# Running sums of logs and angles: one fp32 product against products of ones with two 12-bit halves

## The chip, the cores and the metric

The kernel runs on one core of a Trainium2 chip. The metric is the time of one execution in device microseconds; three executions of the kernel before gave 684.42, 684.94 and 685.08 us, median 684.94. The profile shown is one further execution of 683.65 us, of which the profiler's span is 681.9 us. All times inside the kernel are microseconds from the start of that span.

## The reference

A gated linear attention with complex gates is followed by a layer of two matrix products around a gate h cos(h).

```python
# q, k, v, a_re, a_im: (4, 8, 768, 48) fp32; w_in: (384, 2048), w_out: (2048, 384)
mag = np.sqrt(a_re * a_re + a_im * a_im)
scale = np.minimum(mag, 0.999) / (mag + 1e-06)
a_re_n, a_im_n = (a_re * scale, a_im * scale)
for t in range(S):                       # S = 768 steps
    ar, ai = (a_re_n[:, :, t, :, None], a_im_n[:, :, t, :, None])
    new_re = ar * S_re - ai * S_im       # the state is turned and shrunk
    new_im = ar * S_im + ai * S_re
    kv = np.einsum('bhd,bhe->bhde', k[:, :, t], v[:, :, t])
    S_re, S_im = (new_re + kv, new_im)
    y[:, :, t] = np.einsum('bhd,bhde->bhe', q[:, :, t], S_re)
# (B,H,S,D) -> (B*S, H*D): x of 3072 x 384
h = x @ w_in
g = h * np.cos(h)
out = (g @ w_out).astype(np.float32)
```

## The kernel before

The 768 steps of a batch are cut into six chunks of C = 128 steps. Within a chunk the product of all gates up to a step is exp(running sum of log magnitudes), turned by the running sum of angles. Both running sums are matrix products with a triangle of ones, 128x128, against the chunk's 128x384 logs or angles. Two chunks make a group g; there are 24 chunks and 12 groups. Groups 0 and 1 (g < PEG) take one path, groups 2 to 11 the other, in which the rows of a chunk are stored turned by one step.

The names that the profile uses: `lg` are the logs, `tan` the angles, `lgs` and `phs` the running sums in PSUM, `P` (stored over `lg`) and `Q` their exponentials, `ks` and `qs` the rotated keys and queries, `sc` the scores, `sp` the new state, `yp` the attention output, `hp` the product with `w_in`, `op` and `sum` those with `w_out`.

```python
# the constants: a triangle of ones, and the same over pi, for each of the two paths
sums = [constant(sums_np[0], "sums")]
turns = [constant(sums_np[0] * np.float32(1.0 / math.pi), "turns")]
# ... (later, for g >= PEG)
sums.append(constant(sums_np[1], "sums_turned", nc.sync))
turns.append(constant(sums_np[1] * np.float32(1.0 / math.pi), "turns_turned", nc.sync))

# log_steps, its end: the last writes of the log and the angle, and a check of the sign of re
    special(out=rs, in_=rs, func=AF.Ln, scale=EPS, bias=one_b)
    special(out=sq, in_=mag, func=AF.Ln)
    special(out=sq, in_=sq, func=AF.Exp, scale=-1.0)
    vector.tensor_tensor(out=m2, in0=m2, in1=rs, op=ALU.subtract)        # m2 is lg
    vector.tensor_tensor(out=mag, in0=mag, in1=sq, op=ALU.mult)          # sq is tan
    vector.scalar_tensor_tensor(out=sq, in0=mag, scalar=2.0, in1=sq,
                                op0=ALU.subtract, op1=ALU.mult)
    vector.scalar_tensor_tensor(out=sq, in0=sq, scalar=-1.0, in1=im,
                                op0=ALU.mult, op1=ALU.mult)
    scalar.activation(out=junk, in_=re, func=AF.Relu, scale=-1.0, accum_out=...)

def p_powers(g, i):                       # one chunk of the logs
    ps = pa.tile([C, DM], F32, tag="a", name="lgs")
    matmul(ps, lhsT=sums[g >= PEG], rhs=cut(x["lg"], i, 1), start=True, stop=True)
    special(out=cut(x["P"], i, 1), in_=ps, func=AF.Exp)
    special(out=cut(x["Q"], i, 1), in_=ps, func=AF.Exp, scale=-1.0)

def p_even(g, i, n):                      # "mag<-Q,lg", "lg<-mag,lg", "Q<-mag,Q"
    vector.scalar_tensor_tensor(out=u, in0=Q, scalar=HUGE, in1=P, op0=ALU.min, op1=ALU.mult)
    for t in P, Q:
        vector.scalar_tensor_tensor(out=t, in0=u, scalar=3.0, in1=t,
                                    op0=ALU.subtract, op1=ALU.mult)
    # ... two DMAs

def p_apply(g, i, n):                     # "Q<-k,Q", "mag<-q,lg"
    vector.tensor_tensor(out=Q, in0=cut(x["k"], i, n), in1=Q, op=ALU.mult)
    vector.tensor_tensor(out=u, in0=cut(x["q"], i, n), in1=P, op=ALU.mult)

def g_carry(g, i):                        # the end of the chunk before, added to row 127
    n, some = g * G + i, ds(C - 32, 32)
    if g >= PEG and n % NCH:              # not where a batch begins
        head = cut(X[g]["tan"], i, 1)[some]
        vector.scalar_tensor_tensor(out=head, in0=before(n)[some], scalar=carry[some],
                                    in1=head, op0=ALU.mult, op1=ALU.add)

def g_phase(g, i):                        # one chunk of the angles
    ps = pa.tile([C, DM], F32, tag="a", name="phs")
    early = g < PEG and n % NCH
    if i:
        g_carry(g, i)
    matmul(ps, lhsT=turns[g >= PEG], rhs=cut(x["tan"], i, 1), start=True, stop=not early)
    if early:
        matmul(ps, lhsT=last, rhs=before(n), start=False, stop=True)
    ph = cut(x["tan"], i, 1)
    scalar.copy(out=ph.bitcast(I32), in_=ps)                             # whole turns
    vector.tensor_tensor(out=ph, in0=ps, in1=ph.bitcast(I32), op=ALU.subtract)
```

`prods` of a group runs p_powers for both chunks, the arctangent of the angles (g_angle), g_carry for the first chunk, then p_even and p_apply. `phases` runs g_phase for both chunks, `keys` the sines, the rotations and the transposes of keys and queries, which go through DMA to `kT` and `qT`. `weave` sets the program order: each part gives its pieces places between two fractions, and the pieces are sorted by them. Turn n of the main loop works on the chunks of group n, the products of groups n-1 and n, and prepares group n+1:

```python
for n in range(2, NG):
    weave((mixes(n - 1, 2, 4), 0.0, 0.12), (logs(n + 1), 0.0, 0.02), (chunks(n), 0.0, 0.36),
          (second(n - 1, 0), 0.0, 0.38), (products(n - 1, 0, 3), 0.0, 0.36),
          (prods(n + 1), 0.22, 0.24), (second(n - 1, 1), 0.4, 0.56),
          (products(n - 1, 3, 7), 0.4, 0.56), (phases(n + 1), 0.4, 0.56),
          (keys(n + 1), 0.53, 0.66), ..., (first(n), 0.56, 1.0), ...)
```

`first` is hp, `second` and `products` are op and sum, `chunks` holds sc, sp and yp. The scheduler keeps matmuls in the order of the program; on the other engines it decides.

Of the kernel before, what the change touches and what calls it, by code (L numbers as in the profile page):

```python
# [11 lines left out]
F32 = mybir.dt.float32  # L12
U8 = mybir.dt.uint8
U32 = mybir.dt.uint32
I32 = mybir.dt.int32
BF16 = mybir.dt.bfloat16
I64 = mybir.dt.int64
AF = mybir.ActivationFunctionType
ALU = mybir.AluOpType
# [467 lines left out]
def fast_path(ctx, tc, q, k, v, a_re, a_im, moe_w_in, moe_w_out, out, least, odd, wide):  # L487
# [41 lines left out]
    last_np[C - 1] = 1.0  # L529
    carry_np = np.where(step_np == C - 1, np.float32(math.pi), np.float32(0.0))[:, None]  # L530

    def constant(array, name, queue=nc.scalar):
        t = consts.tile(list(array.shape), F32, name=name)
        queue.dma_start(out=t, in_=nc.inline_tensor(array, name=name + "_const").ap())
        return t

# [31 lines left out]
    for names in ("re", "im"), ("k", "q"), "v":  # L568
        for i in range(G):
            load(0, names, i)  # L570
    ident = constant(np.eye(C, dtype=np.float32), "ident")
    sums = [constant(sums_np[0], "sums")]
    turns = [constant(sums_np[0] * np.float32(1.0 / math.pi), "turns")]
    last = constant(last_np, "last")
    carry = constant(carry_np, "carry")
    causal = constant(causal_np * np.float32(0.25), "causal")
    tiny_b = scalar_tile(TINY, "tiny_b")
# [70 lines left out]
    def chain(ins, engine="scalar"):  # L648

        if engine in tail:  # L650
            behind(ins, tail[engine])
        tail[engine] = ins
# [29 lines left out]
    def matmul(out, **kw):  # L682
        chain(nc.tensor.matmul(out, **kw), "tensor")  # L683
# [30 lines left out]
    def cut(t, i, n):  # L714
        return (flat(t) if len(t.shape) == 4 else t)[:, ds(i * DM, n * DM)]

    def log_steps(g, i, n):


        x = X[g]  # L720
        re, im = cut(x["re"], i, n), cut(x["im"], i, n)
        if i == 0:
            if g == 0:
                x["sin"] = temp("tan", 2)
            for name in "lg", "tan", "rs", "mag":
# [18 lines left out]
        yield  # L744
        vector.tensor_tensor(out=m2, in0=m2, in1=rs, op=ALU.subtract)
        yield
        vector.tensor_tensor(out=mag, in0=mag, in1=sq, op=ALU.mult)
        vector.scalar_tensor_tensor(out=sq, in0=mag, scalar=2.0, in1=sq,
                                    op0=ALU.subtract, op1=ALU.mult)
        vector.scalar_tensor_tensor(out=sq, in0=sq, scalar=-1.0, in1=im,  # L750
                                    op0=ALU.mult, op1=ALU.mult)
        yield
        junk = msb.tile([C, DM], BF16, tag="below", name="below", bufs=1) if n == 1 else rs
        scalar.activation(out=junk, in_=re, func=AF.Relu, scale=-1.0,
                          accum_out=odd[:, ds(next(odds), 1)])

    def g_log(g, i, n):
        for _ in log_steps(g, i, n):
            pass

    def p_powers(g, i):

        x = X[g]
        if i == 0:
            x["P"], x["Q"] = x["lg"], temp("Q")
            x["row"] = rows_d.tile([G * DM], F32, tag="row", name="row")
            x["end"] = ft.tile([D2, G * H], F32, tag="end", name="end")
        ps = pa.tile([C, DM], F32, tag="a", name="lgs")
        matmul(ps, lhsT=sums[g >= PEG], rhs=cut(x["lg"], i, 1), start=True, stop=True)
        special(out=cut(x["P"], i, 1), in_=ps, func=AF.Exp)  # L770
        special(out=cut(x["Q"], i, 1), in_=ps, func=AF.Exp, scale=-1.0)

# [34 lines left out]
    def before(n):  # L807
        return cut(X[(n - 1) // G]["tan"], (n - 1) % G, 1)

    def g_carry(g, i):  # L810

        n, some = g * G + i, ds(C - 32, 32)
        if g >= PEG and n % NCH:
            head = cut(X[g]["tan"], i, 1)[some]
            vector.scalar_tensor_tensor(out=head, in0=before(n)[some], scalar=carry[some],
                                        in1=head, op0=ALU.mult, op1=ALU.add)

    def g_phase(g, i):

        x, n = X[g], g * G + i  # L820
        ps = pa.tile([C, DM], F32, tag="a", name="phs")
        early = g < PEG and n % NCH
        if i:
            g_carry(g, i)
        matmul(ps, lhsT=turns[g >= PEG], rhs=cut(x["tan"], i, 1), start=True, stop=not early)
        if early:
            matmul(ps, lhsT=last, rhs=before(n), start=False, stop=True)
        ph = cut(x["tan"], i, 1)
        scalar.copy(out=ph.bitcast(I32), in_=ps)
        vector.tensor_tensor(out=ph, in0=ps, in1=ph.bitcast(I32), op=ALU.subtract)  # L830

# [298 lines left out]
    def prods(g):  # L1130
        if not 0 <= g < NG:
            return
        for i in range(G):
            yield lambda i=i: p_powers(g, i)
        yield lambda: g_angle(g, 0, G)
        yield lambda: g_carry(g, 0)
        yield lambda: (p_even(g, 0, G), p_apply(g, 0, G))

    def logs(g):
# [4 lines left out]
    def phases(g):  # L1144
        return [lambda i=i: g_phase(g, i) for i in range(G)] if 0 <= g < NG else []
# [15 lines left out]
    def second(g, i):  # L1161
        return [lambda j0=j0: mm2(g, i, j0, 4) for j0 in range(0, NJ, 4)] if g < PLAIN else []
# [19 lines left out]
    after = consts.tile([1, 1], F32, name="after")  # L1182
    wait_for(X[0]["im"][0:1, G - 1, 0, 0:1])
    load(1, ("re", "im", "k", "q"))
    sums.append(constant(sums_np[1], "sums_turned", nc.sync))
    turns.append(constant(sums_np[1] * np.float32(1.0 / math.pi), "turns_turned", nc.sync))
    early = [weight(dst, src) for dst, src in into[:RAW]]
    Ordered.by_hand = True
    preload("natural_log_exp_and_others")
    busy(12)  # L1190
# [20 lines left out]
    for t in (turned(0, 0, "kT") + turned(0, 0, "qT") + early[:1]  # L1211
# [13 lines left out]
          (logs(2), 0.3, 0.31), (chunks(1), 0.7, 1.0), (prods(2), 0.85, 0.87))  # L1225
    room.close()
    stage.update(pool=ctx.enter_context(tc.tile_pool(name="late", bufs=1)), bufs=1)
    weave((second(0, 1), 0.0, 0.35), (phases(2), 0.0, 0.1), (keys(2), 0.1, 0.4),
          (first(1), 0.4, 1.0))
    for n in range(2, NG):  # L1230
        weave((mixes(n - 1, 2, 4), 0.0, 0.12), (logs(n + 1), 0.0, 0.02), (chunks(n), 0.0, 0.36),
              (second(n - 1, 0), 0.0, 0.38), (products(n - 1, 0, 3), 0.0, 0.36),
              (prods(n + 1), 0.22, 0.24), (second(n - 1, 1), 0.4, 0.56),
              (products(n - 1, 3, 7), 0.4, 0.56), (phases(n + 1), 0.4, 0.56),
              (keys(n + 1), 0.53, 0.66), (quarters() if n == PLAIN else [], 0.4, 0.9),
              (last_quarter() if n == PLAIN else [], 0.9, 1.0), (first(n), 0.56, 1.0),
              (mixes(n, 0, 2), 0.9, 1.0), (guarded(n - 1, per) if n > 3 else [], 0.1, 0.9))
# [77 lines left out]
```

## Time and profile before

| what | value |
|---|---|
| median of three executions | 684.94 us |
| span of the profile | 681.9 us |
| mean granted TensorE clock | 0.987 |
| TensorE time of four lgs records (two products) in the chain | 1.29 us |
| ScalarE activation of 128x768, typical | 0.84 us |
| VectorE two-operand fp32 instruction of 128x768 | 0.95 us |
| VectorE carry, 32x384 | 0.618 us, 17 of them |
| hp of successive groups starts at (n=2 to 5) | 174.43, 225.55, 277.97, 328.77 us |

PE is TensorE's matmuls, PEld its weight loads, which overlap them; DVE is VectorE, ACT ScalarE, POOL GpSimd, SP the queue that issues most DMAs. A share of busy time is an average over the span. In lists of instructions a line gives the start, the duration, the engine, the operation with output and inputs, and in square brackets the time for which the engine stood idle before it and what it then waited for. The chain that ended last is followed back from the last instruction, at each step to what released it.

### The profile page before, as it was taken

The numbers are of one execution on the slowest core, as the hardware profiler recorded it, in microseconds if no ns is written. First come the engines' busy times: TensorE is split into PE (matmuls) and PEld (weight loads), VectorE is DVE, ScalarE is ACT, GpSimd is POOL, SyncE is SP. The second block draws the span as 40 slices with busy tenths as digits, with TensorE's granted clock in tenths as the row PEclk, the third lists the DMA queues.
The fourth block names the chain that finished last, engine by engine and source line by source line (L and its number), as shares of the span: only waits on it lengthen the run. The fifth ranks groups of instructions, "written<-read, shape, count | busy, mean of one in ns | idle before, by whom it ended". The sixth has DMA issues, their size and how long they took to land.

```text
span 681.9 us, 10685 instructions
## 1 busy us (share of the span) xinstructions
PE 653.7 (96%) x4060; PEld 577.7 (85%) x4060; DVE 480.3 (70%) x782; ACT 382.5 (56%) x710; POOL 27.3 (4%) x45
## 2 busy tenths in 40 slices
PE   5788999999999999999999999999999999999996
PEld 5686676886899889899899889999899889999895
DVE  4889988468867877777777777767777768762251
ACT  5769784473474475466476476366466467332330
POOL 2012000000000000000000000000000000000000
PEclk8979999999999999999999999999999999999998
DMA  9777717706537557656657657565766653264000
GB/s 245 177 232 230 187 59 159 201 1 143 160 70 140 153 126 164 170 131 154 184 127 158 180 128 161 158 145 122 205 139 130 196 128 83 104 141 127 24 6 24
DMA packets 232954, 94.97 MB, mean 139 GB/s; under 512 B 208814, under 2 KB 221361, under 8 KB 232892
## 3 DMA queue, kind: packets, MB, share of 16 engines
q1 hardware_dynamic: 226396, 68.68, 44.6%
q0 software_dynamic: 5632, 25.17, 11.0%
q8 instruction: 34, 0.56, 0.4%
q10 hardware_dynamic: 864, 0.33, 0.2%
q14 instruction: 28, 0.23, 0.1%
HBM read 69.35 MB, written 24.81 MB: 138 GB/s over the span
## 4 chain that ended last, share of the span: by engine, by line
PE 84%; DMA 5%; DVE 5%; ACT 4%; issue 1%; DVEq 0%; ACTq 0%
PE hp L683 31%; PE op L683 17%; PE sum L683 15%; PE sc L683 6%; PE yp L683 5%; PE sp L683 3%; PE lgs L683 2%; DMA raw<-in_moe_w_out_dram 2%; PE phs L683 2%; DMA qT<-moved 2%; DVE w_in L672 1%; ACT raw L672 1%; DVE w_out L672 1%; PE yr L683 1%; DMA im<-in_a_im_dram 1%
## 5 line engine op out<-in xcount | busy, mean ns | idle before, releaser
L683 PE MATMUL hp<-xT,w_in 128*128 128x256 f32 x1152 | 253.6, 382 | 0.6 <-ACT xT L672 0.6
L683 PEld LDWEIGHTS hp<-xT,w_in 128*128 128x128 f32 x1152 | 220.1, 191 | 32.2 <-ACT xT L672 1.0
L702 ACT ACTIVATE gate<-hp,half_pi_b 128x512 f32<-128x512 f32 x96 | 65.9, 687 | 126.6 <-PE hp L683 126.6
L672 DVE TENSOR_TENSOR gate<-hp,gate 128x512 f32<-128x512 f32 x96 | 65.6, 683 | 60.0 <-ACT junk L672 60.0
L683 PE MATMUL op<-w_out,gate 128*128 128x192 f32 (+1 forms) x448 | 101.6, 375 | 2.3 <-DVE w_out L672 2.3
L683 PEld LDWEIGHTS op<-w_out,gate 128*128 128x128 f32 x448 | 75.8, 190 | 22.5 <-DVE w_out L672 3.5
L672 ACT ACTIVATE junk<-hp 128x512 bf16<-128x512 f32 x96 | 56.6, 590 | 0.0
L683 PE MATMUL sum<-t_s,s 128*128 128x192 f32 x320 | 55.3, 326 | 0.0
L683 PEld LDWEIGHTS sum<-t_s,s 128*128 128x128 f32 x320 | 52.6, 190 | 0.0
L683 PEld LDWEIGHTS sc<-qT,kT 96*128 96x128 f32 x384 | 47.5, 192 | 5.3 <-issue 2.8
L683 PE MATMUL sc<-qT,kT 96*128 96x128 f32 x384 | 49.5, 276 | 2.4 <-DMA qT<-moved 1.3
L672 DVE TENSOR_TENSOR atm<-sc,causal 128x512 f32<-128x512 f32 x48 | 32.8, 686 | 21.3 <-PE sc L683 21.1
L672 ACT ACTIVATE ot<-sum 128x192 f32<-128x192 f32 x30 | 9.5, 321 | 59.8 <-PE sum L683 59.8
L672 DVE SCALAR_TENSOR_TENSOR ot<-op,ot 128x192 f32<-128x192 f32 x31 | 11.0, 355 | 41.2 <-ACT ot L672 26.1
L698 ACT ACT_TABLE_LOAD x26 | 33.4, 1283 | 4.0 <-DMA ident<-ident_const 3.6
L683 PE MATMUL yp<-atm,v 128*48 128x128 f32 x352 | 33.5, 277 | 0.0
L683 PEld LDWEIGHTS sp<-v,ks 128*96 128x96 f32 x320 | 29.7, 165 | 1.8 <-issue 1.0
L683 PE MATMUL sp<-v,ks 128*96 128x48 f32 x320 | 29.6, 245 | 0.0
L683 PE MATMUL sum<-w_out,gate 128*128 128x192 f32 x160 | 29.6, 329 | 0.0
L683 PE MATMUL yp<-qT,state 96*48 96x128 f32 x304 | 29.6, 272 | 0.0
L683 PE MATMUL op<-t_a,gate 128*128 128x192 f32 x160 | 29.0, 332 | 0.0
L672 ACT CAST tan<-phs 128x384 int32<-128x384 f32 x24 | 11.5, 479 | 30.8 <-PE phs L683 30.6
(123 smaller groups left out, 949.2 us busy)
## 6 DMA issues: line engine op xcount, KB each, us to landing
moved<-tr SPq DMA_DIRECT2D x20, 768.0 KB
raw<-in_moe_w_in_dram POOLq DMA_DIRECT2D x16, 768.0 KB, 5.7
raw<-in_moe_w_out_dram POOLq DMA_DIRECT2D x16, 768.0 KB, 4.9
kT<-moved SPq DMA_DIRECT2D x40, 192.0 KB
qT<-moved SPq DMA_DIRECT2D x10, 768.0 KB
k<-in_k_dram SPq DMA_DIRECT2D x24, 192.0 KB
q<-in_q_dram SPq DMA_DIRECT2D x24, 192.0 KB
v<-in_v_dram SPq DMA_DIRECT2D x24, 192.0 KB
```

The lines of the kernel that those rows point to most:

```text
L672: ins = getattr(self.engine, op)(**kw)
L683: chain(nc.tensor.matmul(out, **kw), "tensor")
L698: chain(nc.scalar.preload_act_table_set(table))
L702: chain(nc.scalar.activation(func=func, **kw))
```

## The change

For groups 2 to 11 each fp32 product with the triangle is replaced. The right operand is split into two halves: `hi`, which ScalarE writes as float32r [...], and `lo`, the rest, which VectorE writes by subtraction. Both are multiplied, in float32r, with an exact triangle of ones (`exact`), and added in PSUM; the factor 1/pi of the angles moves from the triangle into the split. A product in float32r is meant to need one pass of the array. For the second chunk of a group the angles of the first are added as well, through a matrix of all ones (`alls`), so that its carry falls away; the carry of the first chunk stays, ahead of the split. The check of the sign of `re` writes its unused output over `re`, because `hi` takes the buffer `rs`. The places of `prods` and `phases` in the main loop are moved later, some constants move to a pool that is given back, and one constant falls away.

```diff
-    ident = constant(np.eye(C, dtype=np.float32), "ident")
-    sums = [constant(sums_np[0], "sums")]
+    ident = constant(np.eye(C, dtype=np.float32), "ident", pool=stage["pool"])
+    sums = [constant(sums_np[0], "sums", pool=stage["pool"])]
 ... (turns and last likewise)
+    def halves(g, x, i, n, scale, part=slice(0, C)):
+        hi, lo, all_ = (cut(t, i, n)[part] for t in (X[g]["hi"], X[g]["lo"], x))
+        scalar.activation(out=hi, in_=all_, func=AF.Copy, scale=scale)
+        vector.scalar_tensor_tensor(out=lo, in0=all_, scalar=scale, in1=hi.bitcast(F32),
+                                    op0=ALU.mult, op1=ALU.subtract)
+    def new_halves(g):
+        for name, tag in ("hi", "rs"), ("lo", "lo"):
+            X[g][name] = gt.tile([C, G * DM], F32R, tag=tag, name=name)
+    def g_halves(g):
+        if g >= PEG:
+            new_halves(g)
+            halves(g, X[g]["lg"], 0, G, 1.0)
+    def summed_up(ps, g, i, name, ones):
+        if g < PEG:
+            matmul(ps, lhsT=ones, rhs=cut(X[g][name], i, 1), start=True, stop=True)
+            return
+        chunks_ = range(i + 1) if name == "tan" else [i]
+        terms = [(half, c) for half in ("hi", "lo") for c in chunks_]
+        for half, c in terms:
+            matmul(ps, lhsT=exact if c == i else alls, rhs=cut(X[g][half], c, 1),
+                   start=((half, c) == terms[0]), stop=((half, c) == terms[-1]))
 ... (p_powers)
-        matmul(ps, lhsT=sums[g >= PEG], rhs=cut(x["lg"], i, 1), start=True, stop=True)
+        summed_up(ps, g, i, "lg", sums[0])
 ...
-    def g_carry(g, i):
-        n, some = g * G + i, ds(C - 32, 32)
+    def g_carry(g):
+        n, some = g * G, ds(C - 32, 32)
 ...
+        if g >= PEG:
+            new_halves(g)
+            halves(g, X[g]["tan"], 0, G, 1.0 / math.pi)
 ... (g_phase)
-        if i:
-            g_carry(g, i)
-        matmul(ps, lhsT=turns[g >= PEG], rhs=cut(x["tan"], i, 1), start=True, stop=not early)
-        if early:
+        if not early:
+            summed_up(ps, g, i, "tan", turns[0])
+        else:
+            matmul(ps, lhsT=turns[0], rhs=cut(x["tan"], i, 1), start=True, stop=False)
             matmul(ps, lhsT=last, rhs=before(n), start=False, stop=True)
 ... (prods: g_halves(g) comes ahead of p_powers)
+    ones = constant(sums_np[1], "sums_turned", nc.sync, stage["pool"])
+    exact = consts.tile([C, C], F32R, name="exact")
+    alls = consts.tile([C, C], F32R, name="alls")
+    chain(nc.gpsimd.tensor_copy(out=alls, in_=one_b.to_broadcast([C, C])), "gpsimd")
     early = [weight(dst, src) for dst, src in into[:RAW]]
+    chain(nc.gpsimd.tensor_copy(out=exact, in_=ones), "gpsimd")
 ... (the turn that prepares group 2)
-    weave((second(0, 1), 0.0, 0.35), (phases(2), 0.0, 0.1), (keys(2), 0.1, 0.4),
+    weave((second(0, 1), 0.0, 0.35), (phases(2), 0.2, 0.3), (keys(2), 0.3, 0.45),
 ... (the main loop)
-              (prods(n + 1), 0.22, 0.24), (second(n - 1, 1), 0.4, 0.56),
-              (products(n - 1, 3, 7), 0.4, 0.56), (phases(n + 1), 0.4, 0.56),
+              (prods(n + 1), 0.28, 0.32), (second(n - 1, 1), 0.4, 0.56),
+              (products(n - 1, 3, 7), 0.4, 0.56), (phases(n + 1)[:1], 0.48, 0.48), (phases(n + 1)[1:], 0.52, 0.52),
```

More of the change, by code (lines that the diff above doesn't have):

```diff
@@ L15 @@
 I32 = mybir.dt.int32
+F32R = mybir.dt.float32r
 BF16 = mybir.dt.bfloat16
@@ L530, in fast_path, with constant @@
     carry_np = np.where(step_np == C - 1, np.float32(math.pi), np.float32(0.0))[:, None]
-    def constant(array, name, queue=nc.scalar):
-        t = consts.tile(list(array.shape), F32, name=name)
+    def constant(array, name, queue=nc.scalar, pool=consts):
+        t = pool.tile(list(array.shape), F32, name=name)
         queue.dma_start(out=t, in_=nc.inline_tensor(array, name=name + "_const").ap())
@@ L570, in fast_path @@
             load(0, names, i)
-    ident = constant(np.eye(C, dtype=np.float32), "ident")
-    sums = [constant(sums_np[0], "sums")]
-    turns = [constant(sums_np[0] * np.float32(1.0 / math.pi), "turns")]
-    last = constant(last_np, "last")
+    ident = constant(np.eye(C, dtype=np.float32), "ident", pool=stage["pool"])
+    sums = [constant(sums_np[0], "sums", pool=stage["pool"])]
+    turns = [constant(sums_np[0] * np.float32(1.0 / math.pi), "turns", pool=stage["pool"])]
+    last = constant(last_np, "last", pool=stage["pool"])
     carry = constant(carry_np, "carry")
@@ L752, in log_steps @@
         yield
-        junk = msb.tile([C, DM], BF16, tag="below", name="below", bufs=1) if n == 1 else rs
+        junk = stage["pool"].tile([C, DM], BF16, tag="below", name="below", bufs=1) if n == 1 else re
         scalar.activation(out=junk, in_=re, func=AF.Relu, scale=-1.0,
@@ L808, in before @@
         return cut(X[(n - 1) // G]["tan"], (n - 1) % G, 1)
-    def g_carry(g, i):
-        n, some = g * G + i, ds(C - 32, 32)
+    def g_carry(g):
+        n, some = g * G, ds(C - 32, 32)
         if g >= PEG and n % NCH:
-            head = cut(X[g]["tan"], i, 1)[some]
+            head = cut(X[g]["tan"], 0, 1)[some]
             vector.scalar_tensor_tensor(out=head, in0=before(n)[some], scalar=carry[some],
                                         in1=head, op0=ALU.mult, op1=ALU.add)
+        if g >= PEG:
+            new_halves(g)
+            halves(g, X[g]["tan"], 0, G, 1.0 / math.pi)
     def g_phase(g, i):
@@ L1132, in prods @@
             return
+        yield lambda: g_halves(g)
         for i in range(G):
@@ L1135, in prods @@
         yield lambda: g_angle(g, 0, G)
-        yield lambda: g_carry(g, 0)
+        yield lambda: g_carry(g)
         yield lambda: (p_even(g, 0, G), p_apply(g, 0, G))
@@ L1184, in fast_path @@
     load(1, ("re", "im", "k", "q"))
-    sums.append(constant(sums_np[1], "sums_turned", nc.sync))
-    turns.append(constant(sums_np[1] * np.float32(1.0 / math.pi), "turns_turned", nc.sync))
+    ones = constant(sums_np[1], "sums_turned", nc.sync, stage["pool"])
+    exact = consts.tile([C, C], F32R, name="exact")
+    alls = consts.tile([C, C], F32R, name="alls")
+    chain(nc.gpsimd.tensor_copy(out=alls, in_=one_b.to_broadcast([C, C])), "gpsimd")
     early = [weight(dst, src) for dst, src in into[:RAW]]
+    chain(nc.gpsimd.tensor_copy(out=exact, in_=ones), "gpsimd")
     Ordered.by_hand = True
```

## The prediction

> **What bounds the kernel now.** I read the busy shares first, then the slices, then single stretches, and last the order in time of one turn of the main loop. The page's busy line and two of its slice rows:
>
> ```profile
> PE 653.7 (96%) x4060; PEld 577.7 (85%) x4060; DVE 480.3 (70%) x782; ACT 382.5 (56%) x710; POOL 27.3 (4%) x45
> ...
> PE   5788999999999999999999999999999999999996
> ...
> PEclk8979999999999999999999999999999999999998
> ```
>
> After the first four slices TensorE is full at full clock. Busy time per stretch says how full (columns: stretch, its length, then busy us of PE, PEld, DVE, ACT, POOL, the clock, DMA share, GB/s); the second row is one turn of the main loop, n=4:
>
> ```profile
> 97.00:121.40 24.40, 23.17 (x165) 16.97 (x165) 22.03 (x31) 13.19 (x22) 0.00 (x0) 1.00 0.59 123
> ...
> 246.40:298.50 52.10, 52.06 (x344) 47.59 (x344) 38.89 (x63) 30.27 (x57) 1.87 (x3) 1.00 0.64 153
> ```
>
> In n=4 TensorE idles 0.04 us of 52.10, so a microsecond taken from TensorE is a microsecond of the kernel, and so is one in which it is made to wait. VectorE (38.89) and ScalarE (30.27) have room on average. What the change touches are the running sums lgs and phs (tile view; ns are minimum, median, maximum), and what they take is in the chain that ended last (start, us, what):
>
> ```profile
> L683 PE MATMUL lgs<-lg,sums_turned x40: 484/486/488, 102.5 to 569.3; 128*128 128x384 f32 x40
> ...
> L683 PE MATMUL phs<-tan,turns_turned x40: 486/486/590, 108.4 to 584.4; 128*128 128x384 f32 x40
> ...
> 258.93 1.29 PE lgs L683 x4
> ```
>
> 40 records for 20 matmuls: each fp32 product shows as two records, and four records for two products occupy 1.29 us, so one 384-column fp32 product takes 0.645 us. The 486 ns are latency; the pace is 322 ns a record.
>
> [...] 0.645 us for 384 columns is four times 0.161. No run so far shows the reduced form. [...] So a product that waits for its right operand holds up all behind it. The trace agrees in the stretch from 97 to 121.4, where TensorE stops at two phs products while other products stand behind them:
>
> ```profile
> 108.43 0.91 PE L683 MATMUL phs<-tan,turns_turned 128*128 128x384 f32 x2 [0.41 <-DVE tan L672]
> ...
> 112.75 0.91 PE L683 MATMUL phs<-tan,turns_turned 128*128 128x384 f32 x2 [0.82 <-DVE tan L672]
> ```
>
> **Part 1, the products.** Only groups 2 to 11 change, ten of them. Before, each has four fp32 products: 4 x 0.645 = 2.58 us. After, lgs has hi and lo for two chunks (4 passes), phs has 2 for the first chunk and 4 for the second, [...]. Saved 0.96 us a group, 9.6 us in all. A weight load of 128 columns is hidden: sc records, each with as many columns of weights, come every 0.112 us (16 in 1.79 us)[...].
>
> **Part 2, the halves.** Per group ScalarE gets two Copy of 128x768 (0.84 us each, as the other 768-wide activations) and VectorE two subtractions of 128x768 (0.95 us as the other 768-wide ones, 0.87 from start to start). VectorE loses one carry of 0.62. That is +1.7 us on 30.3 and +1.3 on 38.9 per turn: throughput is there. Latency is the question, because both lie in the chain log, sum, Exp, carry, sum.
>
> **Part 3, the walk through n=4.** The lines of before that time it, by engine:
>
> ```profile
> 258.77 1.45 PE L683 MATMUL lgs<-lg,sums_turned 128*128 128x384 f32 x4
> ...
> 268.67 0.81 PE L683 MATMUL phs<-tan,turns_turned 128*128 128x384 f32 x2
> ...
> 262.05 0.94 DVE L672 SCALAR_TENSOR_TENSOR mag<-Q,lg 128x768 f32<-128x768 f32 x1
> ...
> 264.37 0.62 DVE L672 SCALAR_TENSOR_TENSOR tan<-tan,carry 32x384 f32<-32x384 f32 x1
> ...
> 267.23 0.95 DVE L672 TENSOR_TENSOR mag<-q,lg 128x768 f32<-128x768 f32 x1
> ...
> 259.61 0.49 ACT L702 ACTIVATE lg<-lgs 128x384 f32<-128x384 f32 x1 [1.16 <-PE lgs L683]
> ...
> 260.74 0.51 ACT L702 ACTIVATE Q<-lgs 128x384 f32<-128x384 f32 x1
> ```
>
> Before, lgs starts at 258.77 and phs at 268.67, 9.9 us later; the carry is long done (264.37 + 0.62). The built order of the changed kernel puts lgs behind sp, yp and half of op (t_a), and then 4 op, 8 sum, 8 op products before phs. Call the start of lgs t.
> - TensorE reaches the lo pass of the first phs at 0.64 (lgs) + 1.30 + 2.60 + 2.60 + 0.16 = t + 7.30.
> - The operand: the first Exp starts 0.2 after the first chunk's sums (259.61 against 259.41), so at t + 0.52; the fourth 1.13 later (t + 1.65); the next VectorE step 0.54 after that (as 312.87 to 313.41 in n=5), t + 2.19. In this turn VectorE's order is mag, lg, Q, carry, Q<-k, mag<-q, and only then lo<-tan: 0.99 + 0.88 + 0.99 + 0.64 + 0.87 + 0.87 + 0.95 = 6.19, done at t + 8.4. hi waits for the carry and finishes on ScalarE near t + 6.7.
>
> So TensorE stands 1.1 us, and the next sum product, which waits for ot<-sum queued behind lo, another 0.1. The turn's gain of 0.96 is gone. This is what I expect in groups 4, 5 and 8, whose built order is this one. In groups 7 and 10 the carry comes earlier and lo ahead of Q<-k: about 0.3 lost. In groups 6 and 9 there is no carry (a new batch begins): lo is ready near t + 6.3, nothing lost. In group 11 yp lies between lgs and phs, 1.9 us more room; about 0.2 lost at lgs. In group 3 twelve op products of 0.645 = 7.7 us lie between, no loss.
>
> Group 2 is apart (97 to 121). lgs stands where it did, but its operand now needs hi, which ScalarE reaches only about 102.4 (Relu, Exp and a copy are ahead of it); lo follows near 103.4 where TensorE wants it at 102.6: 0.8 lost. The stops at phs shown above, with the empty time around them 1.4 us, go, as phs moves behind twelve op products. But phs then ends near 117 and not 113.5; VectorE does the rotation and both transposes until about 127, and the fourth hp tile must wait for a PSUM buffer that VectorE frees after that: 0.9 lost. On balance 0.3 lost.
>
> **Sum.** 9.6 saved; lost 3 x 1.2 + 2 x 0.35 + 0.2 + 0.3 = 4.8. Net 4.8 us: 684.9 - 4.8 = 680.1, I say 680.0. The start (to 97 us) changes by two small GpSimd copies and one 64 KB constant less; I count nothing.
>
> **Rivals.**
> 1. No new wait: 675.3. For it: VectorE is only 75% busy, the products were moved later, evidently to make room, and removing the second carry relieves VectorE in the middle. Against it: the 8.4 against 7.3 above, from measured durations and the built order.
> 2. Waits larger than counted, lgs included: if hi or lo comes later by another microsecond in every turn, all is eaten and it ends at 685 to 688. For it: ScalarE's guard activations (1.02 us) stand ahead of hi in some turns. Against it: most groups have 1 us or more at lgs (in n=4 lo is ready near 262.3, wanted at 263.6).
> 3. The reduced form isn't one pass. At two passes a product, ten cost 3.2 us a group against 2.58: 6 us more, about 691. At four, about 720. Against it: [...] nothing would then be gained by the split.
> 4. Transfers set the end of each turn: sc at the head of a turn waits for DMA qT in three turns, 1.6 us in all. From the last phs to sc stand the same 8 sum and 48 hp products as before, and the chain to qT starts at the same product, so a shorter head shifts both. I expect this wait unchanged within 1 us in all.
>
> **Range and chances.** 675.5 is rival 1; 684.5 is the waits nearly doubled. A gain over 2% means under 671.2, more than the whole saving: 0.03. A loss over 2% (above 698.6) needs rival 3 with four passes, or a large new wait: 0.04.
>
> **What would show it.** lgs and phs matmuls on hi and lo as one record each, about 0.16 us apart. In the waits of PE: phs behind DVE lo, about 1 us each in the turns of groups 4, 5, 8 (near 212-224, 264-276 and 420-432), none in 6 and 9. Periods from hp to hp about 1 us shorter for groups 6 and 9, unchanged for 4, 5, 8. The pair of phs waits near 108 to 113 gone. Wrong would be: f32r records 320 ns apart; no wait at phs in groups 4, 5, 8; or TensorE waiting at lgs in every turn.

## The result, and the profile after

The changed kernel takes 688.81 us, median of four runs (687.66 to 690.31), against 685.01 us for the kernel before on the same chip: ratio 1.0056, 95% interval 1.0033 to 1.0079. Run again later (run 13), on another chip, it took 688.92 us, ratio 1.0070 (1.0048 to 1.0093). So it is slower by 0.6%, where 0.7% faster was predicted.

Below, "turn n" runs from the first scores product sc of group n to that of the next group. Its head ends at the first product hp; its tail is the rest. The sums lgs and phs in the head of turn n belong to group n+1.

The page of the changed kernel: busy times, and the shares of the chain that ended last:

```profile
PE 647.9 (94%) x4080; PEld 579.6 (84%) x4080; DVE 490.8 (71%) x792; ACT 396.5 (58%) x730; POOL 28.3 (4%) x47
...
PE 60%; DMA 12%; DVE 10%; ACT 10%; issue 5%; SPq 2%; ACTq 0%; DVEq 0%
```

TensorE has 5.8 us less to do (653.7 before), but the span grew by 4.7, from 681.9 to 686.6. TensorE's share of the chain fell from 84% to 60%, and transfers, VectorE and ScalarE took the rest: TensorE now waits for others. The two stretches that the prediction showed, turn 1's head and turn 4 (columns as there):

```profile
98.39:121.57 23.18, 22.72 (x172) 17.75 (x171) 18.28 (x26) 14.89 (x25) 0.00 (x0) 1.00 0.57 116
246.63:299.77 53.14, 51.66 (x347) 47.77 (x347) 40.38 (x64) 32.06 (x60) 1.88 (x3) 1.00 0.61 150
```

Turn 4 has 0.40 us less TensorE work and is 1.04 us longer; idle time went from 0.04 to 1.48. The cheap products are there. The tile view of lgs, and the order in time on TensorE in turn 4:

```profile
L684 PE MATMUL lgs<-hi,exact x20: 333/380/473, 104.4 to 577.3; 128*128 128x384 f32 x20
...
L684 PE MATMUL lgs<-lo,exact x20: 334/336/443, 105.3 to 577.4; 128*128 128x384 f32 x20
```

```profile
263.47 0.47 PE L684 MATMUL lgs<-hi,exact 128*128 128x384 f32 x1
263.78 0.34 PE L684 MATMUL lgs<-lo,exact 128*128 128x384 f32 x1
263.95 0.34 PE L684 MATMUL lgs<-hi,exact 128*128 128x384 f32 x1
264.13 0.34 PE L684 MATMUL lgs<-lo,exact 128*128 128x384 f32 x1
264.30 1.46 PE L684 MATMUL op<-t_a,gate 128*128 128x192 f32 x8
...
270.67 0.47 PE L684 MATMUL phs<-hi,exact 128*128 128x384 f32 x1
272.26 0.45 PE L684 MATMUL phs<-lo,exact 128*128 128x384 f32 x1 [1.13 <-DVE lo L673]
```

One record a product, not two, and 0.174 us from start to start. The record of the first pass starts early: the op record ahead of it starts at 263.44, only 0.03 us sooner, where such records are 0.16 apart, and its own successor comes after 0.31. So the four lgs passes hold up what follows by 0.70 us (from 263.44 to 264.30, less 0.16 for that op record), where two fp32 products took 1.29. And there is the stop at phs that the prediction's walk ended in. From TensorE's list of waits (us in total, times, longest); those for lo, hi and xT are new, the "issue" in front of sc was 0.2 and the wait of sc for qT 1.3 before (hp also waits 1.0 us for a gate, which is new):

```profile
PE phs L684 <- DVE lo L673: 3.8, 4, 1.1
...
PE sc L684 <- issue: 2.3, 1, 2.3
PE sc L684 <- DMA qT<-moved: 2.1, 3, 1.0
...
PE hp L684 <- DMA xT<-x: 1.0, 3, 0.5
PE lgs L684 <- DVE lo L673: 1.0, 2, 0.5
...
PE phs L684 <- ACT hi L673: 0.8, 1, 0.8
```

The "issue" is sc at the end of turn 9, where qT lands last; I count it with qT. By parts of the span, measured at first starts of sc and hp: the start up to turn 1 is 2.03 us longer (98.39 against 96.36), the ten heads together 0.91 shorter, the nine tails after the first 3.34 longer and the first 0.61 longer, what follows the last hp 0.4 shorter. Heads were predicted to give 4.8, tails and start nothing. Turns 3 to 9:

| turn | head before | head after | tail before | tail after |
|---|---|---|---|---|
| 3 | 30.41 | 30.82 | 21.05 | 20.72 |
| 4 | 31.36 | 31.90 | 20.73 | 21.24 |
| 5 | 30.08 | 29.82 | 20.72 | 20.82 |
| 6 | 30.41 | 32.09 | 21.28 | 21.74 |
| 7 | 31.37 | 31.78 | 20.72 | 21.87 |
| 8 | 29.98 | 29.18 | 20.72 | 20.72 |
| 9 | 30.41 | 30.11 | 21.82 | 23.27 |

In turns 1, 2 and 10 the heads are 1.70, 0.84 and 0.08 us shorter. A tail with no wait is 20.72 us. The heads of turns 8 and 2, which hold no wait, show the true saving of a group: 0.80 and 0.84 us.

### The profile page after: what moved, and what is told of

Read it like the earlier page. It is cut to its first block, busy times and chain, and to the rows that moved or that the text cites. A ratio compares the mean times of both kernels' runs of the same rounds, so it can differ in the third digit from the quotient of the medians.

```text
span 686.6 us, 10765 instructions
## 1 busy us (share of the span) xinstructions
PE 647.9 (94%) x4080; PEld 579.6 (84%) x4080; DVE 490.8 (71%) x792; ACT 396.5 (58%) x730; POOL 28.3 (4%) x47
## 4 chain that ended last, share of the span: by engine, by line
PE 60%; DMA 12%; DVE 10%; ACT 10%; issue 5%; SPq 2%; ACTq 0%; DVEq 0%
PE hp L684 27%; PE op L684 11%; PE sum L684 8%; PE sc L684 4%; PE yp L684 4%; DMA qT<-moved 3%; DMA raw<-in_moe_w_in_dram 3%; DMA raw<-in_moe_w_out_dram 2%; PE sp L684 2%; DMA xT<-x 2%; PE phs L684 2%; ACT lg L703 2%; SPq L904 1%; DVE lg L673 1%; DVE Q L673 1%
## 5 line engine op out<-in xcount | busy, mean ns | idle before, releaser
L673 ACT COPY yT<-yp 48x512 f32<-48x512 f32 x44 | 25.3, 576 | 21.7 <-PE yp L684 21.3
```

The source lines that it names most:

```text
L673: ins = getattr(self.engine, op)(**kw)
```

## The experiments

Some names first: `xT` is the attention output transposed, which hp reads; `moved` is a step in DRAM between the transposes and kT and qT; `row` and `end` carry the last row of P; the guards are checks of the weights on VectorE and ScalarE, with fetches of their own. `behind(a, b)` puts instruction a behind b in the order of the queue. The diffs are shortened to what bears on the argument.

Three theories at first. A: lo is late at phs, and this costs what is missing. B: lgs now runs some 4 us later against hp (19.0 us ahead of it before, 15.1 in turn 4 after), so the row of P, Q<-k and mag<-q are later on VectorE, with them the k and q loads that these release on SyncE's queue, and these hold up or slow xT, kT and qT. C: the sign check's Relu, in its new place on ScalarE, costs the 2 us at the start. All runs compare with the kernel before on the same chip.

**1. phs later (A).** Both phs behind one more block of products:

```diff
-(phases(n + 1)[:1], 0.48, 0.48), (phases(n + 1)[1:], 0.52, 0.52),
+(phases(n + 1), 0.52, 0.52),
```

> The changed kernel with one edit: in the main loop the first chunk's running sum of angles moves behind the next eight sum products, right ahead of the second's, so that 2.6 us more lie between the lgs products and the first phs. Theory A (TensorE stands at phs because lo comes too late, and that time is lost): the four waits of phs behind lo and hi (0.94, 1.13, 0.76 + 0.80, 0.94 us) vanish and with the wait for ot<-sum behind them some 4.3 us come off, 688.8 to about 684.5. Theory B (each turn is paced by the transfers to qT and xT, and a wait at phs only takes the place of a later one): the waits of sc for qT grow by as much, 687.5 to 689.

689.57 us, ratio 1.0086 (1.0053 to 1.0119). No wait of phs for lo or hi is left, but nothing is won: TensorE stops at sum instead, whose copy ot<-sum stands behind lo on VectorE. Its list of waits:

```profile
PE sum L684 <- DVE ot L673: 5.1, 4, 1.5
```

VectorE's order in time in turn 4 of this run shows why: the copy has three operations of the new group ahead of it.

```profile
270.65 0.96 DVE L673 TENSOR_TENSOR Q<-k,Q 128x768 f32<-128x768 f32 x1
271.52 0.95 DVE L673 TENSOR_TENSOR mag<-q,lg 128x768 f32<-128x768 f32 x1
272.39 0.95 DVE L673 SCALAR_TENSOR_TENSOR lo<-tan,hi 128x768 fp32r<-128x768 f32 x1
273.26 0.35 DVE L673 SCALAR_TENSOR_TENSOR ot<-sum,ot 128x192 f32<-128x192 f32 x1
```

The late operand is a matter of VectorE's queue; moving one product on TensorE gives the wait to the next. In this simple form A falls.

**2. Only the new places.** The kernel before with single precision products and both carries, only prods, phases and keys where the change puts them (for group 2 likewise):

```diff
-(prods(n + 1), 0.22, 0.24), ... (phases(n + 1), 0.4, 0.56),
+(prods(n + 1), 0.28, 0.32), ... (phases(n + 1)[:1], 0.48, 0.48), (phases(n + 1)[1:], 0.52, 0.52),
```

> The kernel before, fp32 products and both carries kept, with the new places of prods, phases and keys alone. Theory B (the later lgs makes row, Q<-k and with them the loads of k, q and v and the copy to xT later, and they meet the transposes on the queue): waits of hp for xT (about 1 us) and of sc for qT (about 3.5 us) appear here too; about 688.5 to 690. Theory A (the waits come from the halves and the moves cost nothing): 684 to 686; in group 2 even up to 1 us better, as the stops at phs near 108 to 113 go.

696.51 us, ratio 1.0167 (1.0150 to 1.0184): the places alone cost 12 us, where the prediction had counted nothing for them. sc waits for qT 6.7 us, up to 2.42. The tails of turns 5, 6, 8 and 9 are 22.45, 23.73, 22.04 and 23.73. So the loss sits where B looks for it, but it is not shown yet that the loads make it.

**3. The Relu of the first two groups** writes to the tile rs, as before:

```diff
-... if n == 1 else re
+... if n == 1 else rs if g < PEG else re
```

> The changed kernel with the unused output of the sign check put back to rs in group 1 only; this alters nothing but the order of ScalarE's instructions near 52 to 62 us. Theory C (the start is 2.0 us longer because with that output in re ScalarE takes a weight conversion, which waits for its load, ahead of the cosine that hp waits for): the scores of group 1 start near 96.4 and not 98.4, total about 686.8. Rival (the start differs by chance from run to run, or by the GpSimd copies): 688.8 and 98.4 as before.

689.20 us, ratio 1.0071 (1.0050 to 1.0092). First sc at 97.63 instead of 98.39, and nothing of it at the end: the waits of hp for xT grew from 1.0 to 2.6 us, those of sc for qT are 3.5 (4.4). C could hold for 0.8 us at most, and not even that is shown: the unchanged kernel, run again, began at 97.66 (run 13).

**4. lgs earlier**, ahead of all eight op products of t_a, 1.3 us sooner:

```diff
-(prods(n + 1), 0.28, 0.32), ...
+(list(prods(n + 1))[:1], 0.25, 0.25), (list(prods(n + 1))[1:3], 0.2701, 0.2701), (list(prods(n + 1))[3:], 0.31, 0.32), ...
```

> The changed kernel with the lgs products ahead of all eight op products with t_a and not in their middle, 1.3 us earlier against the rest. Theory A: phs finds lo nearly ready (8.6 us instead of 7.3 between the two against 8.4 needed), waits at phs under 0.4 us each, at lgs at most 0.3 us each; 4 us less, about 685. Theories A and B together: the loads are 1.3 us earlier too, the waits for qT shrink by a third, about 683.5. If lo<-lg isn't ready so early, the wait only moves from phs to lgs: 688 to 690.

689.42 us, ratio 1.0063 (1.0043 to 1.0082). Waits for xT are gone and tails are shorter (turn 9: 21.74), but lgs now waits for lo in six turns, 5.4 us. A wait is only exchanged. (ScalarE's order in turns 6 and 9 also went back to that of the kernel before, which matters, as told below under theory F; so the shorter tails there are not shown to come from the earlier lgs.)

**5, 6, 8. Three tests of the loads (B).** In 5, SyncE's queue gets xT ahead of row, k and q. In 6, k, q and v are loaded only behind qT. In 8, groups 4 to 11 don't load k and q at all and use group 3's, so the output is not the reference's.

```diff
 (5)  behind(put_row, late["x"]); k, q loads: behind(load, late["x"]); v load ahead of x
 (6)  behind(put_row, late["x"]); k, q, v loads: behind(load, late["qT"])
 (8) +if name in "kq" and g > 3:
     +    X[g][name] = X[3][name]; continue
```

> The kernel after, with only SyncE's queue in another order: the xT move goes ahead of the row and of the k and q loads, the v load ahead of the x move, the output stores behind xT. The k and q loads keep their own releasers (k waits for Q<-k, q for mag<-q), so they still come late. Theory B (late loads collide with the moves of kT and qT): the waits hp<-xT (1.0 us in all) go, the waits sc<-qT (0.4 + 0.75 + 1.0 + 2.3 = 4.4 us) stay within 2 us of that, time 686 to 689. Rival D (it is the queue's order alone, one item holding the next): xT and qT waits both go, 683 to 685.

> The kernel after, with the k, q and v loads of two groups ahead put behind the move of qT on SyncE's queue, so that no load can run beside the moves of kT and qT; xT ahead of the row. Theory B: hp<-xT (1.0 us) and sc<-qT (4.4 us) both fall to under 0.5 us in all, the phs<-lo waits stay at 4.6 us, time 683 to 685. Rival E (qT is late because its producers on VectorE are late, not for the loads): qT waits stay above 3 us, 687 to 689. If the loads now come too late for Q<-k there would be a new wait at the exponentials' products on VectorE, and phs<-lo waits above 6 us.

> The kernel after, with the k and q loads of groups 4 to 11 left out: these groups use group 3's k and q, so the output is not the reference's, and the work on the engines is the same. Theory B: the sc<-qT waits (4.4 us) fall under 0.7 us, the hp<-xT waits (1.0) fall to 0.5 or less, phs<-lo stays at 4.6: 683 to 685. Rival E (producers late on VectorE, not the loads): waits for qT stay above 3 us, 687 to 689.

713.26 us, ratio 1.040 (1.034 to 1.047); 705.09 us, 1.032 (1.028 to 1.036); and 700.78 us with less to load, 1.025 (1.022 to 1.028). All expectations missed: the waits for qT, with "issue", are 16.3, 14.1 and 11.6 us. A kernel with fewer transfers waits longer for a transfer, so the reason must lie ahead of it. In these three runs and in run 2 the last phs ends 2.4 to 2.5 us ahead of hp (3.3 in turn 1 of run 5). Then the sine lg<-tan on ScalarE starts either 1.3 us ahead of hp (2.1 there) or 0.4 to 0.6 us behind it, and rotations, transposes and moves follow it. It is late in eight turns of run 5, in six of run 6, in turns 6 and 9 of run 8, in turns 5, 6, 8 and 9 of run 2, and in turns 6 and 9 of the changed kernel (there at hp, not behind it). Order in time on ScalarE, turn 6, kernel before:

```profile
377.30 0.48 ACT L672 CAST tan<-phs 128x384 int32<-128x384 f32 x1 [0.31 <-PE phs L683]
378.40 0.84 ACT L702 ACTIVATE lg<-tan 128x768 f32<-128x768 f32 x1 [0.62 <-DVE tan L672]
379.15 0.92 ACT L702 ACTIVATE rs<-rs,half_pi_b 128x768 f32<-128x768 f32 x1
379.97 0.31 ACT L672 ACTIVATE ot<-sum 128x192 f32<-128x192 f32 x1
```

and the changed kernel:

```profile
379.64 0.48 ACT L673 CAST tan<-phs 128x384 int32<-128x384 f32 x1 [0.37 <-PE phs L684]
382.25 0.33 ACT L673 ACTIVATE ot<-sum 128x192 f32<-128x192 f32 x1 [2.12 <-PE sum L684]
382.47 0.83 ACT L703 ACTIVATE lg<-tan 128x768 f32<-128x768 f32 x1
383.20 0.92 ACT L703 ACTIVATE rs<-rs,half_pi_b 128x768 f32<-128x768 f32 x1
```

The copy of the last sum has come ahead of the two sines, and it waits 2.12 us, with ScalarE empty, for TensorE to finish a product that the sine has no use for. ScalarE did not take the sine first: its operand tan was written by 380.71 (VectorE, 380.15 + 0.56), and the sine, behind the copy, starts at 382.47. Nobody wrote this order: the program is built by a scheduler that fixes each engine's queue, and the change moved its choice in two turns, my experiments in more. In run 5 the first gate also came ahead of the transpose of ks (5.5 us after hp instead of 3.1), in run 8 SyncE got kT ahead of the second moved in turns 6 and 9. And after long waits (the longest 3.6, 2.7 and 4.8 us) TensorE ran at half clock (told at the end), for 27.3 us in run 5 and 13.7 each in runs 6 and 8; the mean granted clock of these runs is 0.967, 0.978 and 0.974, where the changed kernel has 0.985. Half of these times is lost, an estimate from the clock (run 2 lost 1.67 us in 3.41 at half clock), and no list of waits shows it. These three runs say little on the loads; they tell of these orders. Call it theory F.

**7. lo first.** On VectorE lo<-tan ahead of Q<-k and mag<-q, and the guards of the weights behind the split:

```diff
+behind(Q_k, lo_of_tan); behind(mag_q, lo_of_tan)
+behind(guard_relu, hi_of_tan)
```

> The kernel after, with VectorE's queue in another order only: lo<-tan ahead of Q<-k and mag<-q (behind them in half of the groups), and the guards (raw on VectorE and ScalarE) behind the split of the angles. Theory A2 (phs waits for what is queued on VectorE ahead of lo): phs<-lo waits go from 4.6 to under 1 us. As k and q loads are released by Q<-k and mag<-q, about 1 us later here, theory B says that part comes back as xT and qT waits (5.4 us now, 6 to 8 then): 686 to 688. If theory B is wrong all 4 us are kept: 684 to 685.

702.73 us, ratio 1.027 (1.023 to 1.032). The phs waits are gone as A2 says. In their place hp waits for xT:

```profile
PE hp L684 <- DMA xT<-x: 11.9, 6, 2.5
```

xT stands behind k on SyncE and k behind Q<-k, as B says, but the 11.9 us are more than the 1 us by which Q<-k moved. The guards' fetches moved too, and what xT shared the transfer engines with was not settled. Half clock for 13.7 us (the mean is 0.974) costs, by the same estimate, 6.8 on top; with the phs waits (4.6) gone, this is about the 14 us by which the run is slower than the changed kernel.

**9. The sine first (F).** The changed kernel with one order pinned:

```diff
-scalar.mul(out={...6: c12}[p], in_=ps, mul=scale)
+copied = scalar.mul(out={...6: c12}[p], in_=ps, mul=scale)
+if p == 6:
+    behind(copied, late["sine"])
```

No queue but ScalarE's differs from the changed kernel's, and ScalarE's by two instructions: in turns 6 and 9 the copy stands behind the two sines again.

> The kernel after with two pairs of instructions on ScalarE swapped and nothing else in any queue: in turns 6 and 9 the sine of the angles (lg<-tan) again stands ahead of the last copy ot<-sum, as it does in all turns of before and in the other turns of after. Theory F (a queue order on ScalarE that flipped in two turns makes qT late): the sines of turns 6 and 9 start 1.3 us ahead of the first product hp instead of 0.03, their tails go from 21.74 and 23.27 to about 20.9 and 21.3, the time falls by 2 to 3.5 us against 688.8: 685 to 687. Theory B (late loads): tails 6 and 9 stay within 0.5 us of where they are, 688 to 689.

685.77 us (16 runs), ratio 1.0025 (1.0012 to 1.0039), against 1.0056 and 1.0070 for the changed kernel: 2 to 3 us back. Tails 6 and 9 are 20.82 and 20.83 (21.74 and 23.27), and none is left at "issue". Order in time on ScalarE in turn 6, which ends again as before the change:

```profile
378.73 0.84 ACT L703 ACTIVATE lg<-tan 128x768 f32<-128x768 f32 x1 [0.62 <-DVE tan L673]
...
380.30 0.31 ACT L673 ACTIVATE ot<-sum 128x192 f32<-128x192 f32 x1
```

F holds for these turns: two copies that stand two places too early cost 2 to 3 us of 689. (Tail 7 was 21.87 and is 20.72 here, but so it is in run 3, which has the changed kernel's order in the main loop; that one varies. Tail 9 does not: it is 22.8 to 23.3 us in the four traces with the early copy, the changed kernel and runs 1, 3 and 13, and 20.8 to 22.1 in the five with halves and the sine first, runs 4, 9, 11, 14 and 15.)

**10. The places of run 2 with the sine first.** The same pin; four copies move behind the sines.

> The run that has only the new places (single precision products, no halves; 696.5 us), with the four pairs on ScalarE swapped in which the copy ot<-sum stood ahead of the sine (turns 5, 6, 8 and 9). Theory F: tails 5, 6, 8 and 9 go from 22.45, 23.73, 22.04 and 23.73 to at most 21.3 each, and heads 7 and 10 from 33.03 back to 31.4, as no wait of 2.4 us stands ahead of them any more: 9 to 11 us back, 685.5 to 687.5, so the places themselves cost little. Theory B (late loads): at most 3 us back, 693 or more.

686.75 us, ratio 1.0048 (1.0031 to 1.0065): 2.9 us slower than before on its chip, where run 2 was 11.9 slower, so about 9 us back of the 12. Tails 5, 6, 8, 9: 20.72, 21.48, 20.72, 21.93; heads 7 and 10: 31.36 and 31.37, from 33.03. So the places themselves cost 2 to 3 us, and the rest was the flipped order. The heads show a second price of a wait. A stretch of run 2 (the head of turn 7, right behind a wait of 2.42 us; that of turn 10 is the same), the clock is the column ahead of the DMA share:

```profile
406.56:439.59 33.03, 33.03 (x248) 31.19 (x249) 22.77 (x37) 18.62 (x31) 1.88 (x3) 0.95 0.52 120
```

and of run 10:

```profile
402.43:433.79 31.36, 31.36 (x248) 29.52 (x249) 22.67 (x37) 20.24 (x35) 1.87 (x3) 1.00 0.55 127
```

After the wait the granted clock is lower, 0.95 against 1.00, and the same 248 products take 1.67 us more.

**11 and 15. All orders by hand.** The changed kernel with the sine first, lo first, the transpose of ks ahead of the first gate, end<-end behind it, xT ahead of row, k, q and an output store on SyncE, and keys ending earlier and the guards late in the turn. Run 15 adds the Relu of run 3.

```diff
+behind(copied, late["sine"]); behind(Q_k, lo); behind(mag_q, lo)
+behind(gated, late["turn"]);  behind(ended, late["turn"])
+behind(put_row, late["x"]);   k, q loads: behind(load, late["x"])
-(keys(n + 1), 0.53, 0.66) ... (guarded(n - 1, per), 0.1, 0.9)
+(keys(n + 1), 0.53, 0.60) ... (guarded(n - 1, per), 0.68, 0.95)
```

> The kernel after with all the queue orders that earlier runs pointed to set by hand: ScalarE's sine ahead of ot<-sum, VectorE's lo<-tan ahead of Q<-k and mag<-q, the keys' transpose ahead of the first gate, SyncE's xT ahead of row, k and q, and the guards of the weights in the later part of each turn. Theory F: the waits phs<-lo (4.6), hp<-xT (1.0) and sc<-qT (4.4) fall to 1.5 us in all, so 688.8 less 8 to 9: 679 to 682, which beats both kernels. If loads still collide (theory B), qT waits of 1 to 2 us stay in turns 4 and 7: 681 to 683.

> The run of all queue orders (680.5 us) with the Relu of the first two groups writing to the tile it wrote to in before, as the earlier run did that moved the first scores from 98.4 to 97.6 us. If that part of the start is real: 679.5 to 680.3 us and first scores at 97.5; if the start only varies from run to run, 680 to 681.5.

680.54 us, ratio 0.9956 (0.9940 to 0.9972), and 679.95 us, ratio 0.9931 (0.9908 to 0.9955). Both beat both kernels. From the page and the waits of run 15:

```profile
PE 648.1 (95%) x4080; PEld 581.7 (86%) x4080; DVE 489.6 (72%) x792; ACT 396.5 (58%) x730; POOL 27.7 (4%) x47
```

```profile
PE hp L687 <- DMA xT<-x: 1.4, 1, 1.4
PE phs L687 <- DVE lo L676: 1.2, 2, 0.8
...
PE phs L687 <- ACT hi L676: 1.0, 1, 1.0
...
PE sc L687 <- issue: 0.8, 1, 0.8
```

The arithmetic is the changed kernel's, with 0.2 us of busy TensorE between them, and TensorE's order is the same; 9 us lie in the order of the other queues. Run 9 separates 2 to 3 of them; how the rest divides among the other orders set here, no run shows. Between 11 and 15 the intervals overlap, so the Relu's 0.6 us is not shown.

**12. All orders, loads last.** Run 11 with k, q and v behind qT:

> The same orders, but with the k, q and v loads of two groups ahead behind the move of qT on SyncE's queue. If loads beside the moves of kT and qT are what makes tails 4 and 7 of after 21.2 and 21.9 us long, these tails are 20.7 here and the time is 1 to 1.5 us under that of the other run of all orders; if not, the two are within 0.7 us of each other.

692.23 us, ratio 1.0121 (1.0095 to 1.0147). Missed on both sides: the tails of turns 4 and 7 are 21.1 and 21.6, so no better, and there is a new wait, phs for ScalarE's hi, 6.2 us in three turns. Here loads behind qT are worse than loads beside kT; why hi is late there I have not followed up.

**13 and 14. The changed kernel again, and once more without k and q loads,** this time with the sine first and with the order of moved, kT and qT kept (VectorE's order still differs from run 9's in turn 3):

> The kernel after, unchanged, beside the other two: 687 to 690 us, tails 6 and 9 at 21.5 to 23.5 us. The start of the first scores was 96.6 to 100.3 us in runs with the same order of work at the start, so it may differ by 2 us from the 98.4 of the first trace.

> The kernel after with the sine first on ScalarE in all turns and with the k and q loads of groups 4 to 11 left out (they use group 3's k and q, so the output is not the reference's), and with moved, kT and qT in after's order on SyncE's queue. To compare with the run that has the sine alone (685.8 us). Theory B2 (the loads, as items in the queue and as traffic, make the waits for xT and the tail of turn 4): xT waits 1.9 us there go to 0, the tail of turn 4 goes from 21.74 to 20.8 and all other tails are 20.7 to 20.9; phs<-lo waits stay near 4.4 us; 683 to 684.5. If another traffic does it (re and im loads, guards of the weights): the tail of turn 4 stays over 21.3 us and the time at 685 or more.

688.92 us as told above, with tails 6 and 9 at 21.91 and 23.10. Without the loads 685.24 us, ratio 1.0012 (0.9996 to 1.0028), against 1.0025 (1.0012 to 1.0039) for run 9: the intervals overlap. The waits for xT are gone (1.9 us in run 9) and the tail of turn 4 is 20.99 (21.74), as B2 says, but that of turn 9 is 22.07 and the time is 0.7 us above what B2 allowed. The two runs without the loads have an odd end, though: what follows the last hp takes 47.5 us in runs 8 and 14 and 45.4 to 45.8 in all others, with the last product 39.08 us behind hp as in run 9. These 2 us have nothing to do with waits for xT and qT. From the first sc of turn 1 to the last hp run 14 takes 539.0 us and run 9 539.8. So the loads move single waits, and are worth some 0.8 us by the traces, up to 2.5 by the medians with the end set right; how much it is, these runs do not settle.

## Why the prediction was wrong

**What failed.** Rival 4, in the sentence "a shorter head shifts both. I expect this wait unchanged within 1 us in all". The tails of turns 2 to 10 grew by 3.34 us and hp waited 1.0 us for xT (the 0.61 of tail 1 are foreseen in the walk through group 2). The wait for qT does start at phs, but between phs and qT stands ScalarE's queue, and there a copy had come ahead of the sine in turns 6 and 9. Run 9 undoes just that and gets 2 to 3 us back. The order was in the built program and could be compared turn by turn before any run; I had walked through one turn, and on TensorE and VectorE only. I also asked of the moved places nothing but whether operands would be in time. Run 2 shows that alone they cost 12 us, about 9 of it by the same early copy in four turns. (The wait itself was misread by little: the list before has 0.16, 0.40 and 0.94, 1.5 us and not 1.6.)

This is the largest part, not all. The traces differ from the prediction by 9.5 us (4.7 slower, where 4.8 faster was predicted): 3.3 in these tails, 1.0 in the waits of hp for xT, 2.2 in longer stops for lo and hi, 1.3 in a smaller saving, 2.0 at the start; turn 1, the end and small waits give back 0.4.

**The saving (part 1)** was mis-sized: 0.80 us in turn 8 and 0.84 in turn 2, not 0.96. The prediction took a pass for about a quarter of an fp32 product (0.645 / 4 = 0.161 us), which was my estimate and not shown by a run at that time. A pass takes 0.174 to 0.175 us, 0.27 of the product: the four of lgs hold TensorE for 0.70 us, the two and the four of phs for 0.36 and 0.70, 1.76 in all against 2.58. Over nine groups that is 1.3 us less than predicted. A float32r product is one record at that pace, neither two nor four, so rival 3 falls. Rival 2 named about the right time, 685 to 688, for a reason that is only a part (2.2 us).

**The walk (part 3)** was right where it was done: lo in turn 4 was to be ready 8.4 us after lgs and wanted at 7.3; measured, it ends 8.73 after (271.25 + 0.95 - 263.47), and TensorE stops for 1.13 by the list:

```profile
271.25 0.95 DVE L673 SCALAR_TENSOR_TENSOR lo<-tan,hi 128x768 fp32r<-128x768 f32 x1
```

The stops in the turns that serve groups 4, 5 and 8 are 0.94, 1.13 and 0.94, where 1.2 each was predicted; for 7 it was to be 0.35 and is 0.76 + 0.80, as hi is late too; for 10 it was to be 0.35 and none is listed; for 11 it was to be 0.2 and is 0.52. In group 2 I took the gain at phs for lost again later; the head of turn 1 became 1.70 shorter and its tail 0.61 longer. In sum 5.6 us of listed waits for lo and hi, 0.46 of them in group 2, against 4.5 predicted outside it. The list counts short here: a pass that is followed by the next after 0.17 us has a record of 0.34 to 0.47, and the list counts a wait from the end of the record (in turn 4 from 270.67 + 0.47), so a wait behind a pass is listed some 0.2 to 0.3 us too short. I count from start to start instead. From the start of the product ahead of the first phs to the start of the one behind it 0.52 us pass in turn 8, where nothing is waited for, and 1.72, 1.91, 2.61 and 1.72 in turns 3, 4, 6 and 7: stops of 1.20, 1.39, 2.09 and 1.20. Turn 7 bears this out: a saving of 0.80 and a head 0.41 longer make 1.2. With turn 9 (0.05) and, in the same way at lgs, turn 10 (0.8) the stops outside group 2 are 6.7 us and not 4.5: these are the 2.2 us above, 1.7 of them in turn 6, which the prediction gave 0.35 by analogy with the walk.

**The start** was counted as nothing and is 2 us longer. In the twelve traces with this order at the start the first sc comes between 96.6 and 100.3 us, in the middle at 98.4; without halves (the kernel before, runs 2 and 10) it comes at 96.4 to 96.5. The Relu is not shown to hold any of it (97.63 in run 3 against 97.66 in run 13); the cause stays open.

**Where 680.0 comes back.** With the orders set by hand the kernel takes 680.0 to 680.5 us, the predicted time. That is partly luck: the saving is smaller and the start dearer than I counted in run 11 (98.49), and the phs waits, which I had left in, are mostly gone.

## What to carry to other kernels

A change that moves work in a program whose queues a scheduler fills is also a change of every queue's order. Before judging it, compare each engine's order with the old one for every repetition of the loop, and look for an instruction that waits for something late and now stands ahead of one that feeds the next stage. And an experiment that pins one order must itself be compared so, or it tests another flip: runs 4, 5, 6 and 8 did.

## What the runs showed of the hardware that was not expected

- A short stop of TensorE can cost more than its length, and whether it does depends on where it falls. In the traces of both kernels the granted clock changes only at marks 3.413 us apart or a multiple of that (after: to 0.50 at 44.72 us, 1.00 at 51.54, 0.50 at 68.61, 1.00 at 72.02). Between 100 and 640 us no stretch from mark to mark holds more than 0.94 us of idle TensorE before and 1.51 us after, and the clock stays at 1.00 there. The stop of 2.42 us in run 2 (404.14 to 406.56) is followed by a clock of 0.50 from 407.59 to 411.00, and the next head takes 1.67 us more; that of 2.28 in the changed kernel (558.89 to 561.17) is cut by a mark at 560.13, into 1.23 and 1.05 us, and the clock stays at 1.00. Two stops of 1.02 and 0.80 us (run 15, turn 6, 370.36 to 372.62) end close together, the 16 sum products right behind them take 4.44 us where such products take 2.76, and the clock of that head is 0.95. So 1.51 us of idle time in a stretch had no such consequence, and 1.82 us in two stops had one; where between them it begins, and whether it always does, is not shown.
- float32r passes (fp32r in the trace) of 384 columns follow each other in 0.174 to 0.175 us. Between fp32 products they cost no more than that: four hold TensorE for 0.70 us, though the record of the first starts 0.03 us behind the fp32 record ahead of it and its successor 0.31 later.
